# A delta-rule attention with a GELU network behind it: another eviction for one product, other buffers, zero products and a new written order

## The chip, the core and the metric

The kernel runs on one core of a Trainium2 chip. Five engines work side by side and meet through semaphores: TensorE (PE, with its weight loads shown apart as PEld) multiplies from SBUF into PSUM; VectorE (DVE), ScalarE (ACT) and GpSimd (POOL) do elementwise work, the last without PSUM in this kernel; SyncE (SP) issues most DMAs. The metric is the time of one execution on the device in microseconds.

## The reference

For 4 batches and 8 heads, a state of 48 by 48 is carried over 768 steps, and its output goes through two dense layers.

```python
k_n = k / (np.linalg.norm(k, axis=-1, keepdims=True) + 1e-06)
for t in range(S):
    y[:, :, t] = np.einsum('bhd,bhde->bhe', q[:, :, t], state)
    v_old = np.einsum('bhde,bhd->bhe', state, kt)
    state = state + bt * np.einsum('bhd,bhe->bhde', kt, vt - v_old)
...
h = x @ w_in                       # 3072 x 384 by 384 x 2048
g = 0.5 * h * (1.0 + np.tanh(c * (h + 0.044715 * h * h * h)))
return (g @ w_out).astype(np.float32)
```

Inputs and output are float32; the kernel multiplies in bf16 and sums in float32.

## The kernel before

The 768 steps are cut into 12 chunks of 64 steps. A chunk c has two units of work, u = 2c and 2c+1, of 8 head rows each over 128 partitions (two blocks of 64 steps). Within a chunk the recurrence is solved as a triangular system: a 64 by 64 matrix per head is inverted, first in blocks of 8 by substitution, then by doubling. Names are those of the operations in the code; a number behind the point is the unit or the chunk.

- `load` and `norms` (chunk): the DMAs k, q, v; sq (squares of the keys), sum, pow (square root), eps, inv.
- `prep` (unit): kn (keys scaled to tok), qb (queries cast), vb (values cast); knc, qbc, vbc are the same for a whole chunk. T (or Tk, Tq in the first units) transposes them on TensorE and kT (kTk, kTq) copies that out; `turn` does it by a DMA instead. G (GD, GQ) multiplies keys with keys and queries, dn and wq (or wqa and wqb) copy that out.
- `leaf` (chunk): F gathers the blocks of 8, lp scales by beta, x0 starts the inverse, L spreads, six pairs xm and xa on VectorE do the substitution, xb scales.
- `scale` (unit): xe (or xec for two units) spreads the inverses into zt, KZ multiplies the keys with them, kz copies that out, GM multiplies with the keys, lw copies that out under a mask (line 623).
- `invert` (unit): X10 and X11 put lw into the block matrix bd; product A4, eviction rt4 (added to twice the identity, line 704), product B4, evictions bde40 and bde41 (or xi4 and bdc40, bdc41); product A5, the last but one, its eviction rt5 (line 704 too, 128x256), product B5 for the corners, evictions be50 and be51.
- `chain` (chunk): V and K against the state, R copies, U applies the inverse, Un copies, S and Sn make the next state, Q and O the output, On copies, X and xT (or the DMA turnx) transpose it for the dense layers.
- `mlp` (chunk): 16 products `up` (line 824), four `gelu` on ScalarE (line 828), 8 groups `down` (line 835), evictions Z and stores out.

Nothing here is left to a scheduler at run time: `ORDER` is one list, written out, of all operations in order. Each word names an operation, behind the colon the engine (a, d, g, s for ScalarE, VectorE, GpSimd and SyncE; none is TensorE), behind the @ the PSUM bank of eight. `Flow.order` cuts it into one queue for each engine, and every engine works through its queue in that order; `Flow.emit` adds the semaphore waits that the data, the buffers and the banks ask for. A later operation cannot pass an earlier one on its engine, even one that waits. An operation that the list doesn't name is not emitted: several are declared in two ways (`alt`), and the list takes one.

`const` and `preset` write masks, identities, zero pads and templates (two, sel, rows, tri, ladj, bdz); `warm_up` declares 140 zero products named fill, 128x128 by 128x512, which use a tensor wz of zeros and whose result nobody reads; the list names two. Buffers turn over by number: tok, kT and wq have NP = 6 (three chunks), bd 6, lw and zt 4, the raw inputs 3.

## Time and profile before

| what | before |
|---|---|
| median of 3 runs | 254.16 us (254.01 to 254.86) |
| the profiled execution | 256.58 us, span 254.7 us |
| busy: PE, DVE, ACT, POOL | 226.0, 185.8, 157.4, 130.1 us |
| mean granted clock of TensorE | 0.966 |
| matmuls, weight loads | 5500, 5502 |
| instructions of DVE, ACT, POOL | 445, 244, 159 |

The profile is of one execution. A row of groups gives line, engine, operation, written and read tiles, shapes and count, then the busy time and the mean length of one in ns, then how long the engine was idle before them and what ended that. A row of the timeline gives the start, the length, the engine and the count of the instructions merged. A row of waits gives the total, the number and the longest. A row of windows gives the stretch, its length, the busy time and count for PE, PEld, DVE, ACT and POOL, the granted clock of TensorE (1.00 is full), the busy share of the DMA engines and GB/s. The tile `ps` is PSUM, whatever product stands in it. A busy PE is one with a matmul in flight.

### The profile page before, as it was taken

Reading aid. Unit: us, or ns where it says so; the run is one execution under the profiler, and the core shown is the slowest. Engines: PE = TensorE matmul, PEld = TensorE weight load, DVE = VectorE, ACT = ScalarE, POOL = GpSimd, SP = SyncE. Lnnn points to the kernel's source line nnn. Section 1 sums busy time; section 2 is a strip of 40 time slices with the busy share of each in tenths; the row PEclk is TensorE's granted clock in tenths of the full one; section 3 lists DMA queues with packets and bytes.
Section 4 is the critical chain, followed back from the end, with each engine's and each line's share of the span. In section 5 each row is a group of like instructions: output and inputs, shape, how many; then the busy total and the mean of one; then the engine's idle time right before and its main releaser. Section 6 shows DMA issues by size and latency. Waiting matters only on the chain.

```text
span 254.7 us, 12256 instructions
## 1 busy us (share of the span) xinstructions
PE 226.0 (89%) x5500; PEld 178.3 (70%) x5502; DVE 185.8 (73%) x445; ACT 157.4 (62%) x244; POOL 130.1 (51%) x159
## 2 busy tenths in 40 slices
PE   0259558899999998999999899999999999999994
PEld 0148347687877877777778778787786778678672
DVE  6599989955996989898888779898494665755100
ACT  2637747949568888967647577743866534436261
POOL 7647448347563397627358968472535525330000
PEclk9999956689999999999999999999999999999999
DMA  5986995987785679789678517787359320332042
GB/s 103 165 144 118 184 162 95 165 127 117 128 130 105 112 126 124 135 165 147 119 146 167 100 36 131 147 153 130 56 93 167 62 49 4 33 68 64 3 93 62
DMA packets 104532, 28.25 MB, mean 111 GB/s; under 512 B 98592, under 2 KB 103712, under 8 KB 104480
## 3 DMA queue, kind: packets, MB, share of 16 engines
q1 hardware_dynamic: 99200, 23.79, 54.0%
q0 software_dynamic: 2880, 3.15, 7.8%
q8 instruction: 43, 0.70, 1.2%
q10 hardware_dynamic: 2400, 0.54, 1.1%
q14 instruction: 9, 0.07, 0.1%
HBM read 20.64 MB, written 4.72 MB: 100 GB/s over the span
## 4 chain that ended last, share of the span: by engine, by line
PE 73%; DVE 15%; ACT 4%; DMA 2%; ACTq 2%; issue 2%; SPq 1%; POOL 0%
PE ps L835 24%; PE ps L824 22%; PE ps L692 5%; PE ps L620 3%; PE ps L752 3%; PE ps L773 2%; DMA vraw<-in_v_dram 2%; PE ps L697 2%; PE ps L564 2%; DVE lw L623 2%; DVE xl L658 2%; PE ps L633 2%; PE ps L759 2%; DVE ps L655 2%; PE ps L609 1%
## 5 line engine op out<-in xcount | busy, mean ns | idle before, releaser
L824 PE MATMUL ps<-xT,W 128*128 128x256 bf16 x576 | 76.8, 277 | 0.4 <-DVE xl L658 0.4
L835 PE MATMUL ps<-W,gT 128*128 128x384 bf16 x384 | 72.7, 326 | 0.0
L828 ACT ACTIVATE gT<-ps 128x1024 bf16<-128x1024 f32 x48 | 48.4, 1022 | 26.4 <-PE ps L824 25.8
L824 PEld LDWEIGHTS ps<-xT,W 128*128 128x128 bf16 x576 | 52.2, 99 | 9.3 <-DVE xl L658 0.5
L835 PEld LDWEIGHTS ps<-W,gT 128*128 128x128 bf16 x384 | 34.0, 97 | 18.2
L682 POOL TENSOR_SCALAR_AFFINE_SELECT bd<-lw 64x512 bf16<-64x512 bf16 x34 | 22.6, 667 | 37.7 <-DVE lw L623 28.6
L704 DVE TENSOR_TENSOR rl<-ps,two 128x384 bf16<-128x384 f32 (+1 forms) x48 | 22.9, 484 | 9.7 <-PE ps L692 9.5
L623 DVE CAST_PREDICATED lw<-mlw,ps 128x832 bf16<-128x832 uint16 x24 | 24.3, 1018 | 6.8 <-PE ps L620 6.5
L499 POOL TENSOR_TENSOR nrm<-nrm,half 128x16 f32<-128x16 f32 x9 | 26.6, 2956 | 2.8 <-DVE nrm L497 2.7
L343 ACT ACTIVATE bd<-ps 32x256 bf16<-32x256 f32 (+1 forms) x40 | 16.8, 428 | 8.2 <-PE ps L692 4.4
L692 PEld LDWEIGHTS ps<-lw,bd 128*128 128x128 bf16 x384 | 15.5, 98 | 4.2 <-POOL bd L682 1.2
L692 PE MATMUL ps<-lw,bd 128*128 128x32 bf16 (+1 forms) x384 | 17.2, 183 | 1.2 <-POOL bd L682 1.1
L658 DVE TENSOR_TENSOR xl<-ps,xl 128x96 bf16<-128x96 f32 (+4 forms) x72 | 16.0, 228 | 2.0
L655 DVE TENSOR_TENSOR ps<-ps,xl 128x64 f32<-128x64 f32 (+5 forms) x72 | 15.6, 221 | 2.0 <-PE ps L649 0.5
L343 ACT ACTIVATE ob<-ps 128x384 f32<-128x384 f32 x17 | 8.3, 490 | 14.0 <-PE ps L835 14.0
L722 POOL COPY bd<-xi 64x256 f32<-64x256 f32 x20 | 8.0, 401 | 16.4 <-ACT xi L343 8.5
L540 PE MATMUL ps<-ident,tok 128*128 128x128 bf16 x80 | 7.8, 246 | 8.1 <-POOL tok L531 3.8
L531 POOL TENSOR_TENSOR tok<-kraw,nrm 128x384 bf16<-128x384 f32 x9 | 8.5, 945 | 12.7 <-DVE bsb L349 5.6
L349 ACT ACTIVATE kT<-ps 128x512 bf16<-128x512 f32 x18 | 10.4, 596 | 6.4 <-PE ps L609 6.4
L343 ACT ACTIVATE dn<-ps 128x512 bf16<-128x512 f32 x18 | 10.4, 593 | 5.3 <-PE ps L564 5.3
L620 PE MATMUL ps<-kT 48*64 48x56 bf16 (+1 forms) x768 | 11.1, 196 | 2.8 <-ACT kT L349 1.4
L599 POOL TENSOR_TENSOR zt<-xb,blk 128x2048 bf16<-128x2048 bf16 x3 | 10.9, 3642 | 4.1 <-DVE xb L669 3.9
(132 smaller groups left out, 428.3 us busy)
## 6 DMA issues: line engine op xcount, KB each, us to landing
qraw<-in_q_dram SPq DMA_DIRECT2D x48, 96.0 KB, 3.6
vraw<-in_v_dram SPq DMA_DIRECT2D x48, 96.0 KB, 3.5
kraw<-in_k_dram SPq DMA_DIRECT2D x44, 96.0 KB, 3.6
out_dram<-ob SPq DMA_DIRECT2D x22, 192.0 KB, 3.0
W<-in_moe_w_in_dram POOLq DMA_DIRECT2D x2, 768.0 KB, 8.8
W<-in_moe_w_out_dram POOLq DMA_DIRECT2D x2, 768.0 KB, 9.6
kraw<-in_k_dram ACTq DMA_DIRECT2D x7, 48.0 KB, 3.3
out_dram<-ob SPq DMA_DIRECT2D x3, 96.0 KB, 2.2
```

What stands on the lines that cost most here:

```text
L343: return e.activation(out, in_, ACT.Copy) if e is nc.scalar else e.tensor_copy(out, in_)
L499: if e is nc.scalar else e.tensor_tensor(nr[:, 1, hx], nr[:, 0, hx], half[:, hx], ALU.pow), reads=[nrn, "half"] + ["one"] * (c < ROOTS),
L620: ins = e.matmul(P(ps("GM"))[hf(a), o_ + c0:o_ + c1], kT[s][r, y, g, hf(a)], kT[s][r, z, g, C * a + c0:C * a + c1])
L623: A(("dve",), op("lw"), lambda e, P: e.copy_predicated(lw[m][:, :, 0:LW - LB], mlw[:, :, :].rearrange("p w t -> p (w t)")[:, 16:16 + LW - ...
L655: A(("dve",), f"xm{m}.{c}", lambda e, P, m=m, w=w, part=part: e.tensor_tensor(part(P), P(f"L.{c}")[:, off[m]:off[m] + 2 * H * w].rearrange ...
L658: A(("dve",), f"xa{m}.{c}", lambda e, P, m=m, part=part: e.tensor_tensor(xl[y][:, :, m + 1:LB], part(P), xl[y][:, :, m + 1:LB], ALU.add), ...
L682: A(("pool", "dve"), op(f"X1{a}"), lambda e, P, src=lw[m][hf(a), :, LW - C:LW], dst=bd[b_][hf(a), :, hf(a)], a=a: e.affine_select(out=dst, ...
L692: ins = e.matmul(P(name)[:, C * h + c0:C * h + c1], bd[b_][:, h, :], rhs[:, h, :])
L704: A(("dve",), op(f"rt{i}"), lambda e, P, i=i, c0=c0, c1=c1, r_=r_: e.tensor_tensor(r_[:, 0:H, c0:c1], P(ps(f"A{i}")).rearrange("p (h t) -> ...
L824: ins = e.matmul(P(ph)[:, 256 * f:256 * f + 256].rearrange("p (x t) -> p x t", x=2), W1[:, j, 128 * (i + f):128 * (i + f) + 128], x_[:, :, ...
L828: A(("act",), f"gelu{i // 4}.{c}", lambda e, P, i=i, ph=ph: e.activation(g_[:, i:i + 4, :], P(ph).rearrange("p (f t) -> p f t", f=4), ACT. ...
L835: ins = e.matmul(P(po)[:, 0:DM], g_[:, f, 128 * b:128 * b + 128], W2[:, f, :], start=(f == 0), stop=(f == FC - 1))
```

## The change

- Eviction of the last but one product: rt5 no longer adds twice the identity on VectorE. It multiplies by a sign for each partition (`sign`, −1 and 1 in stripes of 32), as an activation with a scale or a tensor_scalar, so it may stand on ScalarE. The new list has 13 of 24 on ScalarE, 11 on VectorE.
- Sums of squares: a second way is declared, sh and si, which halve 48 columns to 24 and 12 on GpSimd, and su, which sums the rest. The new list names `sum` for every chunk, and none of sh, si and su.
- The squares sq themselves: on ScalarE for all 13 in the old list; in the new one 7 on GpSimd, 3 on VectorE, 3 on ScalarE.
- Buffers: tok, kT and wq for 8 units instead of 6; the keys times inverses (kz) go to zT with 5 buffers instead of a third part of kT; the raw betas lie in the output buffers, so the first outputs wait for the transposes of beta; two scratch tensors of a way of `leaf` that no list used are gone.
- Another way for A4 and rt4 (Ai4, rc4), pairs of chunks in `leaf`, and the two beta evictions on either engine are declared; the list names neither Ai4 and rc4 nor pairs.
- 19 zero products instead of 2: one at the very start, the others between unit 4's transposes and the first output product O.0.
- The list is new: order, engines and banks. Among others GpSimd writes rows1 ahead of the first square; bde41 stands on ScalarE 14 times instead of 8, kz 22 instead of 18, xi4 with its two copies is taken for 8 units instead of 12.
- The DMAs of the inputs are the same, with the same shapes; they stand in the list in another order.

Cut to its core; of the list only the stretches that the prediction speaks of:

```diff
--- before.py
+++ after.py
...
-be51.0:d v2.01:s xe.4:d U.0@0 bde41.3:d KZ.4@4 Un.0:a w2.1:g rt4.2:d kz.4:a O.0@6 sum.3:d A5.3@4 On.0:a S.0@2 rt5.3:d GM.4@0 sq.4:a xe.5:d X.0@6
-B4.2@7 lw.4:d Sn.0:a fill85@4 KZ.5@4 xT.0:a sum.4:d X11.4:g bde40.2:a up4.0@2 kz.5:d pow.3:g up0.0@0 bde41.2:a up1.0 X10.4:d tabG:a up2.0 up12.0@6
...
+bdz1:g mmlw:d beta10:a k1.11:s blk1:d pad7:d rowz:d wz:g bdz0:d k0x1.10:a k0x1.01:s tmplz:g fill136@0 tmpl0:g bdz4:d tmpl1:g k0x1.00:a beta01:s one:g
+mln0:g pad4:d pad3:d blk2:g pad1:d k0x1.11:a q0.11:s pad6:d identf:d pad5:g triwq6:d sign0:d low1:d half:d blk3:g tabS:a k1.10:s mmuq:g beta00:a
+muq0:g k1.01:s pad0:g rows1:g k0x0.00:a beta11:s trilw1:a k1.00:s k0x0.10:a k2.10:s sq.0b:g q0.00:s own:g sum.0b:d k2.11:s ident:d betaT0@0 pow.0b:a
...
+fill131@4 mln1:g xa6.0:d fill51@4 xm6.1:d v0.11:s xb.0:d low2:g Tq.3@5 xa6.1:d xe.1:d wqa.1:a betaS2@7 betaC1:a fill44@4 xe.0:d G.4@2 KZ.1@0 kTq.3:d
+wqb.1:g dn.4:a G.5@4 kz.1:a wq.4:d dn.5:a fill132@0 mwp1:g betaC2:d wqa.5:a GM.1@0 xb.1:g fill114@2 lw.1:d v0.00:s wqb.5:g KZ.0@4 F.2@3 kz.0:a Tq.2@2
+tabG:a sign1:d lp.2:d X10.1:d L.2@3 xe.3:d x0.2:d triwq3:a KZ.3@0 ladj4.0:d GM.0@4 xe.2:d kz.3:a fill43@7 fill46@7 xm1.2:d trilw3:a X11.1:g lw.0:d
+KZ.2@0 k5.10:s fill0@7 fill60@7 fill130@7 kz.2:a xa1.2:d kTq.2:a GM.3@4 sign3:d X11.0:g xm2.2:d k3.10:s fill71@7 xa2.2:d betaC3:a fill95@0 xm3.2:d
+lw.3:d ladj5.0:a X10.0:g k4.11:s k4.01:s A4.1@2 xa3.2:d X11.3:g A4.0@4 xm4.2:d k3.01:s fill42@5 rt4.1:d fill109@5 rt4.0:d k3.00:s X10.3:g B4.1@6
+GQ.2@0 xi4.1:a GM.2@4 k4.00:s vb.1:d B4.0@2 ladj5.1:a xa4.2:d lw.2:d bdc41.1:g vb.0:a v1.00:s bde40.0:a bdc40.1:g V.0@6 v2.01:s bde41.0:a wq.2:d
+A4.3@4 X11.2:g A5.1@5 k4.10:s R.0:a A5.0@2 rt5.1:d fill119@0 X10.2:g rt4.3:d v2.11:s rt5.0:a B5.1@5 fill83@6 xm5.2:d B5.0@0 xa5.2:d w2.0:g q4.00:s
+B4.3@1 xm6.2:d be50.0:a A4.2@4 xa6.2:d bde40.3:d be51.0:a be50.1:a be51.1:a rt4.2:d xb.2:g bde41.3:a U.0@6 w2.1:g xe.4:d fill50@4 Un.0:a GQ.3@2 KZ.4@4
+wq.3:d B4.2@1 kz.4:a fill12@0 qb.7:g O.0@6 vbc.1:d GM.4@4 On.0:a lw.4:d sq.3:g X.0@2 S.0@6 xT.0:d A5.3@4 qb.6:g Sn.0:a up4.0@2 xe.5:d up5.0 up6.0
...
+gelu1.2:a up14.2 eps.6:g out00.1:s up15.2 inv.6:d qb.13:d GM.8@2 gelu3.2:a kn.12:g GM.9@0 lw.8:d KZ.10@6 kn.13:g kz.10:a turn.12:s up8.2@4 sq.7:a
+lw.9:d GM.10@6 X10.8:g KZ.11@2 up9.2 kz.11:a up10.2 X11.8:g lw.10:d vb.9:a up11.2 turn.13:s up0.3@2 gelu2.2:a up1.3 sum.7:d GM.11@0 X10.10:g up2.3
...
+Q.11@6 R.11:a up13.10 B5.22@4 be51.23:a up14.10 be50.22:a down10.10@0 be51.22:a U.11@4 down00.10@1 Un.11:d up15.10 down01.10 gelu3.10:a O.11 down02.10
+On.11:a down03.10 X.11@2 Z0.10:d down11.10 xT.11:a down12.10 down13.10 up0.11@2 Z1.10:a up1.11 up4.11@6 out11.10:s up5.11 up2.11 out00.10:s up12.11@0
...
-    NR, NP, NB, NN, NI, NX, NG, NRL = 3, 6, 6, 4, 3, 3, 3, 2
+    NR, NP, NB, NN, NI, NX, NG, NRL, NZ = 3, 8, 6, 4, 3, 3, 3, 2, 5
+    GROUPS = [[0], [1], [2], [3], [4], [5], [6], [7], [8], [9], [10], [11]]
...
-        braw = sb("braw", [32, NC, 2, C], F32)
+        obs = sb("obs", [128, 4, DM], F32)
+        braw = obs[0:32, :, :].rearrange("p n e -> p (n e)").rearrange("p (c y t) -> p c y t", y=2, t=C)
+        ob = [obs[:, 0:2, :], obs[:, 2:4, :]]
...
-        kT = sb("kT", [128, 3, 4, 128], BF16, NP)
+        kT = sb("kT", [128, 2, 4, 128], BF16, NP)
+        zT = sb("zT", [128, 4, 128], BF16, NZ)
...
+            for i_ in range(4):
+                A(("dve",), f"sign{i_}", lambda e, P, i_=i_: e.memset(sign[32 * i_:32 * i_ + 32, :], 1.0 if i_ % 2 else -1.0), writes=[f"sign{i_}"])
...
-                A(("dve",), f"sum.{z}", lambda e, P, sqx=sqx, nr=nr, hx=hx: e.tensor_reduce(nr[:, 0, hx], sqx, AX.X, ALU.add), reads=[sqn], writes=[nrn])
+                A(("dve",), f"sum.{z}", lambda e, P, sqx=sqx, nr=nr, hx=hx: e.tensor_reduce(nr[:, 0, hx], sqx, AX.X, ALU.add), reads=[sqn], writes=[nrn],
+                  alt=(f"sm.{c}", 0) if c else None)
+                if c:
+                    for n_, d_ in (("sh", D // 2), ("si", D // 4)):
+                        A(("pool",), f"{n_}.{z}", lambda e, P, sqx=sqx, d_=d_: e.tensor_tensor(sqx[:, :, 0:d_], sqx[:, :, 0:d_], sqx[:, :, d_:2 * d_], ALU.add),
+                          reads=[sqn], writes=[sqn], alt=(f"sm.{c}", 1))
+                    A(("dve",), f"su.{z}", lambda e, P, sqx=sqx, nr=nr, hx=hx: e.tensor_reduce(nr[:, 0, hx], sqx[:, :, 0:D // 4], AX.X, ALU.add), reads=[sqn], writes=[nrn],
+                      alt=(f"sm.{c}", 1))
...
-            A(EV, op("kz"), lambda e, P: neg(e, kT[s][:, 2, :, :].rearrange("p g (a t) -> p a g t", a=2), P(ps("KZ")).rearrange("p (a r) -> p a r", a=2)[:, :, 0:4 * C].rearrange("p a (g t) -> p a g t", g=4)),
-              frees=[ps("KZ")], writes=[n("kTz")])
+            A(EV, op("kz"), lambda e, P: neg(e, zT[u % NZ][:, :, :].rearrange("p g (a t) -> p a g t", a=2), P(ps("KZ")).rearrange("p (a r) -> p a r", a=2)[:, :, 0:4 * C].rearrange("p a (g t) -> p a g t", g=4)),
+              frees=[ps("KZ")], writes=[f"kTz{u % NZ}"])
...
+                if i == 5:
+                    A(EV, op("rt5"), lambda e, P, r_=r_: scaled(e, r_[:, 0:H, 0:32], P(ps("A5")).rearrange("p (h t) -> p h t", h=H)[:, :, 0:32], sign[:, 0:1]),
+                      reads=[f"sign{i_}" for i_ in range(4)], frees=[ps("A5")], writes=[rn])
+                else:
+                    A(("dve",), op(f"rt{i}"), lambda e, P, i=i, c0=c0, c1=c1, r_=r_: e.tensor_tensor(
                     r_[:, 0:H, c0:c1], P(ps(f"A{i}")).rearrange("p (h t) -> p h t", h=H)[:, :, c0:c1],
-                    two[:, c0:c1].unsqueeze(1).to_broadcast([128, H, c1 - c0]), ALU.add), reads=["two"], frees=[ps(f"A{i}")], writes=[rn])
+                    two[:, c0:c1].unsqueeze(1).to_broadcast([128, H, c1 - c0]), ALU.add), reads=["two"], frees=[ps(f"A{i}")], writes=[rn], alt=(op("a4"), 0) if i == 4 else None)
```

301 lines of the change are left out of this document (151 added, 150 removed).

## The prediction

> **What bounds the kernel now.** I read the page first, its busy shares and its slices.
>
> ```profile
> span 254.7 us, 12256 instructions
> PE 226.0 (89%) x5500; PEld 178.3 (70%) x5502; DVE 185.8 (73%) x445; ACT 157.4 (62%) x244; POOL 130.1 (51%) x159
> PE   0259558899999998999999899999999999999994
> PEclk9999956689999999999999999999999999999999
> ```
>
> A slice is 6.4 us. From the ninth on TensorE is busy throughout; in the first eight, about 51 us, it is not. There are two stages: a head that builds the first chunks and a body in which one matmul follows the other. The view by windows, cut where the clock changes, tells what each is limited by (columns: length, then busy us of PE, PEld, DVE, ACT, POOL, then the granted clock).
>
> ```profile
> 12.70:22.70 10.00, 6.84 (x153) 5.82 (x154) 9.48 (x28) 4.95 (x10) 4.55 (x7) 1.00 0.78 137
> 22.70:32.90 10.20, 5.93 (x186) 4.68 (x184) 9.79 (x35) 7.73 (x16) 5.31 (x10) 1.00 1.00 165
> 32.90:43.10 10.20, 7.63 (x257) 6.88 (x258) 9.14 (x25) 5.40 (x11) 7.29 (x12) 0.50 0.69 117
> 43.10:46.60 3.50, 2.02 (x81) 1.59 (x79) 3.44 (x8) 3.12 (x6) 2.19 (x3) 0.99 0.92 142
> 46.60:49.90 3.30, 2.89 (x105) 2.66 (x103) 3.30 (x5) 3.23 (x6) 0.54 (x1) 0.50 1.22 180
> 49.90:53.40 3.50, 3.50 (x25) 2.48 (x18) 1.65 (x4) 2.27 (x4) 3.07 (x2) 0.50 1.32 204
> 49.90:63.70 13.80, 13.80 (x248) 10.77 (x240) 8.35 (x17) 9.91 (x15) 8.39 (x7) 0.87 0.83 128
> ```
>
> The head is VectorE's: it is busy 35.2 of the 37.2 us from 12.7 to 49.9. The clock of TensorE is whole up to 32.9, halved to 43.1, whole for 3.5 us, and halved again from 46.6 to 53.4. The page has 1.00 from the start, yet in the chain of waits, in order of time,
>
> ```profile
> 9.00 0.56 DVE nrm L497
> ...
> 15.08 0.62 PE ps L540 x4
> ...
> 24.30 0.46 PE ps L540 x8
> ```
>
> four transposes take 0.62 us at 15 and eight take 0.46 at 24, so the 1.00 of the first 20 us is no record of a full clock. It fell at 46.6 after a stretch in which TensorE was busy 2.02 of 3.50 us, and rose at 53.4 after one in which it was busy all the time. In the body VectorE has room: 8.35 of 13.80 us.
>
> Next come the waits of TensorE alone in the body, and its timeline at both ends of the body.
>
> ```profile
> PE ps L620 <- issue: 0.7, 1, 0.7
> PE ps L620 <- DVE lw L623: 0.7, 1, 0.7
> PE ps L824 <- DVE xl L658: 0.4, 1, 0.4
> PE ps L609 <- ACT gT L828: 0.3, 1, 0.3
> PE ps L609 <- POOL zt L602: 0.3, 1, 0.3
> PE ps L795 <- issue: 0.2, 1, 0.2
> ```
>
> ```profile
> 49.94 3.81 PE L824 MATMUL ps<-xT,W 128*128 128x256 bf16 x18
> ...
> 240.91 5.08 PE L824 MATMUL ps<-xT,W 128*128 128x256 bf16 x45
> 245.82 5.36 PE L835 MATMUL ps<-W,gT 128*128 128x384 bf16 x32
> ```
>
> The first product of the dense part (up4.0, line 824) starts at 49.94 and the last matmul ends at 251.2, 201.3 us later, with 2.6 us of waits between. Behind that lie 3.5 us for the last eviction and store. The time is therefore the start of up4.0, plus the matmul work behind it, plus waits, plus 3.5. One more loss is in the first row: 18 products took 3.81 us at half clock, while 45 took 5.08 at the full one, 0.113 each; 18 of these are 2.0 us. So the cold start of the body costs 1.8 us.
>
> This execution took 256.6 us in all, 1.9 more than its span; the median of the runs, 254.16, is 0.5 below the span. I add up in the span and take that 0.5 off at the end.
>
> **The change, part by part.** Matmul work of the body: the new order issues the same products behind up4.0 with A5.3 done ahead of it and KZ.5 behind, and as many changes between 64-row and 128-row products (96 in both by my count of the two lists). The term stays 201.3 − 1.8 = 199.5 us at full clock, the 2.6 us of waits included.
>
> The head. VectorE bounds it, so I count what its queue has ahead of the first product of the dense part.
>
> ```profile
> 13.06 1.96 DVE L531 TENSOR_TENSOR tok<-kraw,nrm 128x384 bf16<-128x384 f32 x1
> ...
> 14.95 0.54 DVE L531 TENSOR_TENSOR tok<-kraw,nrm 128x384 bf16<-128x384 f32 x1
> ```
>
> ```profile
> 12.63 2.05 POOL L382 TENSOR_SCALAR_AFFINE_SELECT rows<-rows 128x1024 bf16<-128x1024 bf16 x1
> ...
> 32.46 1.01 DVE L623 CAST_PREDICATED lw<-mlw,ps 128x832 bf16<-128x832 uint16 x1
> ...
> 34.79 1.02 DVE L623 CAST_PREDICATED lw<-mlw,ps 128x832 bf16<-128x832 uint16 x1 [0.46 <-PE ps L620]
> ```
>
> ```profile
> L495 ACT ACTIVATE sq<-kraw 128x768 f32<-128x768 f32 x11 | 9.2, 838 | 2.0 <-DMA kraw<-in_k_dram 1.9
> L704 DVE TENSOR_TENSOR rl<-ps,two 128x256 bf16<-128x256 f32 x24 | 10.0, 419 | 6.3 <-PE ps L692 6.0
> L349 ACT ACTIVATE kT<-ps 128x512 bf16<-128x512 f32 x18 | 10.4, 596 | 6.4 <-PE ps L609 6.4
> L343 ACT ACTIVATE bd<-ps 32x256 bf16<-32x256 f32 x29 | 10.4, 368 | 3.6 <-PE ps L697 3.1
> L343 DVE CAST bd<-ps 32x256 bf16<-32x256 f32 x19 | 7.7, 409 | 5.5 <-ACT bd L343 3.1 <-PE ps L697 2.1
> L524 POOL TENSOR_TENSOR tok<-kraw,nrm 128x768 bf16<-128x768 f32 x3 | 4.4, 1477 | 6.8 <-PE ps L824 3.9 <-DVE bd L722 2.3 <-DVE nrm L503 0.6
> L602 DVE TENSOR_TENSOR zt<-xb,blk 128x1024 bf16<-128x1024 bf16 x7 | 4.7, 685 | 0.1
> L343 DVE COPY kT<-ps 128x512 bf16<-128x512 bf16 x6 | 2.3, 416 | 0.3 <-PE ps L540 0.2
> L418 DVE TENSOR_SCALAR rl<-tmpl 128x128 bf16<-128x128 bf16 x1 | 0.7, 655 | 0.0
> L343 DVE COPY wq<-tmpl 128x512 bf16<-128x512 bf16 x1 | 0.5, 510 | 0.0
> L343 DVE CAST vb<-vraw 128x384 bf16<-128x384 f32 x2 | 2.2, 1110 | 0.0
> ```
>
> Out of it go the scaling of keys kn.2, to GpSimd (1.96, of which 0.54 is its own time: it ran through the 2.05 us of GpSimd's rows1); three transposed copies, to ScalarE (3 × 0.42); rt5.0, two corner copies and a block copy of unit 3, to ScalarE (0.42 + 2 × 0.41 + 0.75); sum.3, rt5.3 and xe.5, to behind the first product (2.0); a preset of rl (0.90); and constants and zero fills. Together 12.2 us by each one's own length. In come four presets of wq (4 × 0.51), another of rl (0.65), X10.1, casts of v for chunks 0 and 1 (1.11 + 0.64), betaC2, bde40.3, xT.0 from ScalarE, and constants: 11.0 us. The net is 1.2 us less, with rows1 now ahead of the keys, so that kn.2 need not meet it.
>
> Not all of that arrives. The squares of chunk 0 go to GpSimd behind rows1, and I estimate that the first sum starts near 7.9 instead of 9.0; sel then stands ahead of inv.0b, which eats it again. Followed on through VectorE's queue by these lengths, lw.1 comes about 0.6 us earlier than at 32.46 (lw.0 stood at 34.79). But between lw.1 and lw.0 VectorE now has X10.1, xe.3, a preset of rl, xe.2, xm1.2 besides lp.2 and x0.2: 0.4 + 0.69 + 0.65 + 0.69 + 0.3, some 2.7 us more, in place of a zero fill and a wait of together 0.9; xec.1 (1.2) has gone from ahead of lw.1. Unit 0 loses what unit 1 won. Its later steps win a little again: at full clock its products are shorter, but ScalarE gets rt5.0, both corner copies and the block copy of unit 3 ahead of Un.0, 0.40 + 2 × 0.37 + 0.67, where one corner copy (0.37) and one square (0.84) stood. The price of rt5 on ScalarE is not in the trace: between 0.37 (32x256) and 0.60 (128x512), and by the width I take 0.40, about what VectorE takes; 13 of 24 go there, and in the body TensorE's other work hides them, or at worst 0.2 us each where they stand on a path. Bounds for the start of up4.0: 1.2 earlier (the whole net arrives) and 1.0 later (the order around lw.0 stays on the path). I take 0.4 earlier, 49.5, nearer to the middle since both are argued from the same queue.
>
> The 19 zero products. None has a row; a 256-column product takes 0.113 at full clock and 0.21 at half (the two rows above), so one of 512 columns takes 0.22 to 0.45. Seventeen more are 3.7 to 7.6 us of TensorE's time, where TensorE is idle 11.9 of the 37.2 us from 12.7 on. Three stand together while GM.3 waits for lw.0, so they cost nothing there. Six stand directly ahead of A4, B4 and B5 of units 0 and 1; with their cover gone they would cost up to 6 × 0.45 = 2.7. What they can gain is the clock: they add about 0.5 us of work to each stretch of 3.5 us like the one that fell at 46.6. Ends: nothing, and the 1.8 us of the cold body (with the head's part inside the bounds above). I take 1.8.
>
> The Trainium skill, in TensorE: Matmul & The Clock Gate, Part 1, says that the clock halves after at least one idle window of about 3.4 us and is whole again after a busy one. By that rule the clock would not have fallen at 46.6, and the zero products would buy nothing; the rows show it falling there at 2.02 us busy, so the row decides. The stretches of 10.2, 3.5 and 6.8 us are about three, one and two such windows.
>
> Squares of keys. The halving on GpSimd is written, but the order calls sum, not su, in every chunk, so that part does nothing. What does move are ten of thirteen squares, seven to GpSimd and three to VectorE. ScalarE loses 0.84 for each; GpSimd's price lies between that and 1.48 (its product of two inputs, 128x768), and I take 1.48, the row of the same engine. GpSimd is 51% busy, and the square precedes its key scaling by microseconds, so 0 on the path.
>
> Buffers for four chunks, keys times zeros in a tensor of their own, betas and outputs in one buffer: no wait of TensorE in the body names a reuse of these, so 0, and the outputs' new wait is for a transpose of the first 9 us. Loads stand behind fewer reuses on SP's queue, but no wait of TensorE there names a load; 0. The last steps: KZ.10 to GM.10 now has one group of up between (3 × 0.113), against 0.60 for kz.10, and B5.22 to U.11 one of up and one of down (4 × 0.167, from the 32 in 5.36), 1.0, against two corner copies of 0.37 and their handing over. I add 0.3 each, 0.6 in all.
>
> Sum: 49.5 + 199.5 + 0.6 + 3.5 = 253.1 in the span, 1.6 below 254.7. That makes 252.6 against the median of 254.16.
>
> **The rivals.** First, the clock falls in the same way. For it: the zero products make up 0.5 us in 3.5, and TensorE must wait for VectorE all through the head. Also the clock may become whole later than in the 20 to 24 us of before, since the row of products from 19 on is thinner now. Then 1.8 comes back: 254.4, and with the head's gain gone too 254.8. Chance 0.17 for a time within 0.3% (0.76 us, about what this measurement can tell from no change).
>
> Second, and on the other side: GpSimd's squares hold VectorE up. The row of 1.96 us against 0.54 shows a VectorE instruction with two inputs waiting out a GpSimd one. Five squares of 1.48 (sq.3, 6, 9, 10 and 11) stand from up4.0 on, and the new order has VectorE full there: counted by each one's length, 12.7 us lie in the first 12 us behind up4.0, where 8.35 of 13.80 were busy before. If each square costs VectorE 1.4 and VectorE hands on two thirds, 4.7 us come to TensorE: 257.3. It decides from 2.4 us on. Against it: affine selects and casts of GpSimd stood beside VectorE before, and fewer of these are left. Chance 0.25.
>
> The Trainium skill, in SBUF — State Buffer, section SBUF: two separate sides, says that the two engines share a port pair as an exclusive lock, and whoever comes second waits for the whole instruction. The 1.96 us agrees; by that rule this rival is as priced.
>
> Third, the zero products stand in the way and the clock never holds: 1.8 + 2.7 on top, 257.1. Against it: the products behind them wait for VectorE anyway. Chance 0.13.
>
> **How the numbers follow.** The forecast has 0.45. Faster 0.45, same 0.17, slower 0.25 + 0.13 = 0.38. Its own range is 250.9 to 253.4: 0.8 from the head and 0.9 from waits on either side, the upper end where it meets the first rival. For 8 in 10 the range has to take in most of the slower cases: 250.3 to 257.3.
>
> **What would show it.** The granted clock should be whole from about 27 us on to the end, up4.0 should start near 49.5, and 18 products of line 824 there take 2.0 us. TensorE's waits behind it should sum to about 3 us, and VectorE should be busy over 11 of the 12 us behind up4.0. The prediction is wrong if TensorE's waits in the body exceed 5 us, if up4.0 starts after 51, or if the squares on GpSimd come with VectorE instructions of over 1.5 us.

## The result, and the profile after

The changed kernel takes 260.83 us (median of 4 executions, 260.11 to 260.89), the kernel before beside it 254.28. The ratio is 1.0248, with a 95% interval from 1.0222 to 1.0273: slower, and 3.5 us above the upper end of the range. A later set gave 260.37 against 254.40, 1.0248 again.

The head of the page, after:

```profile
span 258.0 us, 12283 instructions
PE 230.4 (89%) x5519; PEld 175.9 (68%) x5519; DVE 187.4 (73%) x447; ACT 167.0 (65%) x266; POOL 120.3 (47%) x142
PE   1287877898999998999999989989999999999994
PEclk9999999999999999999999999999999999999999
```

The clock row is whole, as forecast; the record of the clock begins at 28 us. The view by windows over the stretches that were shown of before (columns: length, busy us and count of PE, PEld, DVE, ACT, POOL, granted clock, DMA share, GB/s):

```profile
32.90:43.10 10.20, 7.66 (x242) 4.94 (x241) 9.86 (x25) 8.44 (x16) 6.35 (x11) 1.00 0.75 139
43.10:46.60 3.50, 2.28 (x83) 1.84 (x82) 2.66 (x8) 2.90 (x8) 3.40 (x5) 1.00 0.90 136
46.60:49.90 3.30, 2.79 (x120) 2.06 (x117) 3.14 (x5) 2.06 (x4) 2.22 (x3) 1.00 1.27 187
49.90:63.70 13.80, 12.88 (x288) 9.98 (x290) 12.01 (x22) 9.11 (x14) 9.48 (x7) 1.00 0.68 114
```

The clock no longer falls at 32.9 or 46.6. Behind 49.9 VectorE is busy 12.01 of 13.80 us, 8.35 before, and TensorE for the first time idles there. The timeline of TensorE at both ends of the body:

```profile
49.51 0.72 PE L856 MATMUL ps<-xT,W 128*128 128x256 bf16 x5
...
249.13 5.36 PE L867 MATMUL ps<-W,gT 128*128 128x384 bf16 x32
```

The dense part starts at 49.51 (before 49.94), where the forecast had it, and the last matmul ends at 254.5 (before 251.2). So the time was lost in the body. In its first 12 us VectorE is busy 10.2, where the forecast wanted over 11. The waits of TensorE there (total, number, longest):

```profile
PE ps L709 <- DVE rl L725: 1.2, 1, 1.2
PE ps L627 <- ACT gT L860: 1.1, 1, 1.1
PE ps L814 <- issue: 0.8, 2, 0.5
PE ps L639 <- issue: 0.5, 2, 0.2
PE ps L709 <- DVE bd L701: 0.4, 1, 0.4
```

With the smaller ones they come to 5.4 us from up4.0 on, against the 2.6 of before.

To see also what hides in stretched products, I gave every product of the body a price, the median time from its start to the next one's by kind (up 0.33, down 0.65, GM 0.27 and so on, 0.09 more where 64-row and 128-row products meet), and took the rest of the time as loss. The prices sum to 193.7 before and 193.9 after. The losses are 6.8 us in the profiled execution of before, 1.7 of them the half clock, and 10.3 after.

### The profile page after: what moved, and what is told of

Same layout as the page of the kernel before. It is cut to its first block, busy times and chain, and to the rows that moved or that the text cites. A ratio compares the mean times of both kernels' runs of the same rounds, so it can differ in the third digit from the quotient of the medians.

```text
span 258.0 us, 12283 instructions
## 1 busy us (share of the span) xinstructions
PE 230.4 (89%) x5519; PEld 175.9 (68%) x5519; DVE 187.4 (73%) x447; ACT 167.0 (65%) x266; POOL 120.3 (47%) x142
## 4 chain that ended last, share of the span: by engine, by line
PE 69%; DVE 17%; POOL 6%; ACT 5%; issue 2%; POOLq 0%
PE ps L867 22%; PE ps L856 19%; PE ps L709 6%; PE ps L639 3%; PE ps L784 3%; DVE lw L642 2%; PE ps L582 2%; PE ps L805 2%; PE ps L714 2%; ACT bd L352 2%; DVE nrm L508 2%; PE ps L655 2%; PE ps L791 2%; DVE zt L620 2%; POOL nrm L517 1%
## 5 line engine op out<-in xcount | busy, mean ns | idle before, releaser
L604 POOL TENSOR_TENSOR wq<-wq,muq 128x512 bf16<-128x512 bf16 x11 | 13.5, 1227 | 9.8 <-ACT wq L352 9.7
L681 DVE TENSOR_TENSOR ps<-ps,xl 128x96 f32<-128x96 f32 (+5 forms) x72 | 15.5, 223 | 2.6 <-PE ps L675 0.9
L358 ACT ACTIVATE zT<-ps 128x512 bf16<-128x512 f32 x22 | 12.6, 594 | 6.9 <-PE ps L627 6.8
L684 DVE TENSOR_TENSOR xl<-ps,xl 128x96 bf16<-128x96 f32 (+5 forms) x72 | 15.6, 225 | 1.6
L725 DVE TENSOR_TENSOR rl<-ps,two 128x384 bf16<-128x384 f32 x24 | 13.0, 552 | 4.6 <-PE ps L709 4.5
L352 ACT ACTIVATE dn<-ps 128x512 bf16<-128x512 f32 x21 | 12.4, 595 | 4.2 <-PE ps L582 3.9
L508 DVE TENSOR_REDUCE nrm<-sq 128x16 f32<-128x768 f32 (+1 forms) x13 | 11.4, 878 | 3.8 <-POOL sq L507 3.8
L352 ACT ACTIVATE obs<-ps 128x384 f32<-128x384 f32 x16 | 7.8, 490 | 9.2 <-PE ps L867 9.1
L352 DVE CAST bd<-ps 32x256 bf16<-32x256 f32 (+1 forms) x25 | 11.8, 475 | 1.5 <-PE ps L709 0.7
L582 PE MATMUL ps<-kT 48*64 48x128 bf16 (+1 forms) x448 | 11.0, 222 | 1.0 <-DVE rl L425 0.5
```

Source lines behind the costliest of these rows:

```text
L352: return e.activation(out, in_, ACT.Copy) if e is nc.scalar else e.tensor_copy(out, in_)
L508: A(("dve",), f"sum.{z}", lambda e, P, sqx=sqx, nr=nr, hx=hx: e.tensor_reduce(nr[:, 0, hx], sqx, AX.X, ALU.add), reads=[sqn], writes=[nrn] ...
L582: ins = e.matmul(o, kT[s][r, y, g, hf(a)], kT[s][r, z, g, hf(a)])
L681: A(("dve",), f"xm{m}{p}.{c}", lambda e, P, m=m, w=w, part=part: e.tensor_tensor(part(P), P(f"L.{c}")[:, off[m]:off[m] + w2 * w].rearrange ...
L684: A(("dve",), f"xa{m}{p}.{c}", lambda e, P, m=m, part=part: e.tensor_tensor(xl_[:, :, m + 1:LB], part(P), xl_[:, :, m + 1:LB], ALU.add), r ...
```

## The experiments

Ratios are to executions of the kernel before on the same chip. Diffs show a few words of the order on each line.

**The clock of the kernel before.** No edit: a second profile.

> The kernel before, unchanged, profiled a second time, to learn whether the clock falls that were counted as 1.8 us to be won belong to its usual executions. Theory A (they were a mark of that one execution, 256.6 us, and the median of 254.2 has none of them): the granted clock stays whole from about 27 us to the end, the 18 products of line 824 at the start of the dense part take 2.0 us instead of 3.81, up4.0 starts near 49, and the span is about 252.3. Rival B (the falls are in every execution, and the 2.4 us between 256.6 and 254.2 lie elsewhere): the clock is at 0.5 again in the stretches from 32.9 to 43.1 and from 46.6 to 53.4, and the 18 products take 3.8 us again. Time in both: 254.2.

254.45 us, ratio 1.0013 (0.9978 to 1.0049). Its profiled execution, at 255.4 us with a clock of 0.966, had both falls again, and up4.0 at 49.8. But these runs list the clock and span of each execution, and they spread: of 23 of the kernel before, five have 0.966 and a span of 253.4 to 254.5, eighteen have 0.971 to 0.980 and a median span of 252.2. A mean of 0.980 over 252 us leaves 10 us at half clock, as long as the first fall alone; 0.966 leaves 17, both in full. One later profile, of the run before_moved below, is such an execution (clock 0.980). Its windows:

```profile
32.90:43.10 10.20, 7.66 (x264) 6.74 (x263) 9.14 (x25) 5.65 (x11) 7.30 (x12) 0.58 0.57 105
...
46.60:49.90 3.30, 2.43 (x106) 1.99 (x107) 3.30 (x5) 3.29 (x5) 0.60 (x1) 1.00 1.23 175
49.90:53.40 3.50, 3.39 (x64) 2.81 (x62) 2.27 (x7) 3.19 (x5) 3.00 (x2) 1.00 1.31 204
```

The first fall lies from 31.3 to 41.5 here, 1.6 us earlier than in the profile of before, and the second, which the forecast wanted to win back, is not there. Both theories were half right: the falls belong to the kernel, but by the mean clocks the second one comes in full only in a fifth of its executions, and both profiles of the kernel before itself were of that fifth.

**The zero products taken out of the changed kernel.**

```diff
 k0x1.01:s tmplz:g
-fill136@0
 tmpl0:g bdz4:d
...
```

Seventeen fills go in this way; fill83 and fill12 stay.

> The changed kernel without 17 of its 19 zero products (two are left, as before). Theory A (the clock of the kernel before did not fall in its usual executions either, so the zero products buy little): within 0.5 us of 260.8, either way. Rival B (they hold the clock up and are worth the 1.8 us that the forecast gave them): 262.6 or more, with the granted clock at 0.5 in a stretch of the head and in the first microseconds of the dense part. Rival C (they stand in the way, 0.22 us each where TensorE has no wait): 258 to 260.

263.75 us, ratio 1.0361 (1.0320 to 1.0402), clock 0.939 to 0.958. Rival B: they hold the clock and are worth 2.9 us, more than the 1.8 of the forecast. The timeline shows it in the start of the dense part:

```profile
53.34 1.44 PE L856 MATMUL ps<-xT,W 128*128 128x256 bf16 x6
```

The windows show it in the clock, which is half from 32.9 to 43.1 as it was before:

```profile
32.90:43.10 10.20, 7.40 (x227) 6.18 (x226) 8.98 (x22) 8.11 (x16) 5.02 (x9) 0.50 0.77 142
```

Without them the new order starts the dense part at 53.34, 3.4 us later than the old one with its own two zero products. Ahead of that start its clock is half for 18.5 us, against 13.6 before, so the 3.4 are the order and the clock together; no run parts the two. The new head needs its zero products, and they hid what the rest of it cost.

**The squares on GpSimd.** The two longest waits have a common neighbour. The timelines of VectorE, GpSimd and TensorE after, around B4.15 and ahead of KZ.19:

```profile
149.67 1.70 DVE L549 TENSOR_TENSOR tok<-kraw,nrm 128x384 bf16<-128x384 f32 x1
151.29 1.64 DVE L620 TENSOR_TENSOR zt<-xb,blk 128x1024 bf16<-128x1024 bf16 x1
...
149.49 1.47 POOL L507 TENSOR_TENSOR sq<-kraw 128x768 f32<-128x768 f32 x1
150.91 1.47 POOL L604 TENSOR_TENSOR wq<-wq,muq 128x512 bf16<-128x512 bf16 x1
...
153.46 0.41 PE L709 MATMUL ps<-rl,bd 128*128 128x64 bf16 x8 [1.19 <-DVE rl L725]
...
170.58 2.40 DVE L617 TENSOR_TENSOR zt<-xb,blk 128x2048 bf16<-128x2048 bf16 x1
...
170.44 1.47 POOL L507 TENSOR_TENSOR sq<-kraw 128x768 f32<-128x768 f32 x1
```

kn.19 takes 1.70 us (0.54 alone) beside sq.10, xe.16 takes 1.64 (0.69 alone) beside the wqb.16 behind it, and xec.9 2.40 (1.2 alone) beside sq.11. rt4.15 and KZ.19 stand behind them. The waits of the page put KZ.19 down to a gelu, which ended at the same moment, 173.14; xec.9 ended at 172.99. The first experiment:

```diff
 A4.15@3 down00.4@7 rt4.15:d
-sq.10:g
 vbc.7:a up15.5 rt4.14:d B4.15@6 turn.19:s gelu3.5:a
+sq.10:a
...
 xa5.9:d On.7:a
+sq.11:a
...
-sq.11:g
 KZ.19@2 gelu1.6:a
```

> The changed kernel with two of its GpSimd squares, sq.10 and sq.11, on ScalarE. In the profile after, kn.19 takes 1.70 us instead of 0.56 and xe.16 1.64 instead of 0.68 beside and behind sq.10, and xec.9 2.41 instead of 1.22 beside sq.11; TensorE stands 1.36 us ahead of B4.15 and 1.13 ahead of KZ.19. Theory A (the squares stretch VectorE's instructions, and VectorE hands it on to TensorE): these two waits go down to 0.3 or less each, xec.9 takes 1.2 again, and the time is 1.5 to 2.5 us less, 258.3 to 259.3. Rival B (the waits are there for another reason, or others come in their place): within 0.5 us of 260.8, with TensorE still standing over 0.8 us at either place or at the next product that needs VectorE.

257.76 us, ratio 1.0127 (1.0079 to 1.0176), 3.1 us below the changed kernel. The losses at the two products fall from 1.36 and 1.13 to 0.16 and nothing, and xec.9 takes its own time again:

```profile
169.49 1.21 DVE L617 TENSOR_TENSOR zt<-xb,blk 128x2048 bf16<-128x2048 bf16 x1
```

Theory A, with more than its 1.5 to 2.5 us. In a later set, with the changed kernel beside it (below), the difference was only 1.5. In the second experiment the squares stay on GpSimd, at other places:

```diff
-rt4.15:d sq.10:g vbc.7:a
+rt4.15:d vbc.7:a
...
-wqb.16:g B4.14@2
+wqb.16:g sq.10:g B4.14@2
...
-pow.10:g v9.00:s
+pow.10:g sq.11:g v9.00:s
...
-up7.6 sq.11:g KZ.19@2
+up7.6 KZ.19@2
```

> The changed kernel with all its squares still on GpSimd, but two of them at other places in GpSimd's queue: sq.10 behind wqb.16 (about 152.4 us, when VectorE reads PSUM: rt4.14, bde40.15), sq.11 behind pow.10 (about 164.4, beside xm1.9 to xa6.9, which read PSUM too). In the profile after, sq.6 ran at 88.52 beside thirteen such small instructions and none of them was stretched. Theory A (only VectorE instructions with both inputs in SBUF, such as kn and xe, are held up by GpSimd's square): xec.9 takes 1.2 us instead of 2.41, the wait of TensorE at KZ.19 goes, that at B4.15 goes below 0.4, and the time is as with the two squares on ScalarE, 257.3 to 258.5. Rival B (a square on GpSimd costs VectorE its 1.2 us wherever it stands): 260 to 261, with rt4, bde40.15 or the xm and xa of chunk 9 stretched by over 0.5 us.

259.70 us, ratio 1.0164 (1.0092 to 1.0236), and neither forecast. xec.9 was free and the wait at KZ.19 gone, but both squares met others of the same sort. Timelines of GpSimd and VectorE:

```profile
150.14 1.78 POOL L507 TENSOR_TENSOR sq<-kraw 128x768 f32<-128x768 f32 x1
164.03 1.46 POOL L507 TENSOR_TENSOR sq<-kraw 128x768 f32<-128x768 f32 x1
...
150.52 1.95 DVE L620 TENSOR_TENSOR zt<-xb,blk 128x1024 bf16<-128x1024 bf16 x1
164.18 1.44 DVE L662 SCALAR_TENSOR_TENSOR xl<-lp,unit 128x112 bf16<-128x112 bf16 x1
165.66 0.27 DVE L681 TENSOR_TENSOR ps<-ps,xl 128x96 f32<-128x96 f32 x1
```

wqb.16 had moved up, and sq.10 with it, to xe.16 (1.95 us), and B4.15 lost 1.29. sq.11 met x0.9, 0.33 us long alone, now 1.44; the chain of xm and xa behind it came as much later, and B4.17 lost 1.12. The instruction after x0.9, which reads PSUM, took its usual 0.27, but it began when the square was over and decides nothing. In the changed kernel itself sq.6 ran from 88.52 to 89.98 beside a row of these, and none was longer than alone:

```profile
88.52 1.47 POOL L507 TENSOR_TENSOR sq<-kraw 128x768 f32<-128x768 f32 x1 [3.48 <-DMA kraw<-in_k_dram]
...
88.68 0.24 DVE L684 TENSOR_TENSOR xl<-ps,xl 128x80 bf16<-128x80 f32 x1
```

So it is not the square alone that costs, but the square, or another product of GpSimd, beside a VectorE instruction with both inputs in SBUF. The Trainium skill, SBUF — State Buffer, section SBUF: two separate sides, names just this pair (two SBUF inputs on VectorE against a GpSimd operation that reads SBUF) and says that the later one waits for all of the earlier. The rows agree: kn, xe, xec and x0 grow by 0.9 to 1.3 us, the instructions with an input in PSUM by nothing.

**The wait for a power.** pow.3 on GpSimd runs from 52.07 to 55.66, VectorE's next instruction is eps.3, and VectorE stands from 54.22 to 55.69; A4.4 and A4.5 then lose 0.31 and 0.61.

```diff
-xT.0:d A5.3@4
+xT.0:d sum.3:d A5.3@4
...
-rt5.3:d KZ.5@6 X11.4:g sum.3:d kz.5:a up0.0@4
+rt5.3:d X11.4:g up0.0@4
...
-up3.0 up7.0
+up3.0 KZ.5@6 kz.5:a up7.0
```

> The changed kernel with sum.3 ahead of xe.5, X10.4 and rt5.3 in VectorE's queue, right behind xT.0 (KZ.5 and kz.5 a few products later to make room). In the profile after, sum.3 starts at 51.05, pow.3 on GpSimd runs from 52.07 to 55.66, and VectorE stands from 54.22 to 55.69 because eps.3 is next in its queue; A4.4 and A4.5 then come 0.31 and 0.61 late. Theory A (VectorE waiting in line for that power is what holds TensorE there): eps.3 waits under 0.4 us, the two losses go below 0.3 together, and the time is 0.6 to 0.9 less, about 260.0. Rival B (VectorE simply has too much to do behind up4.0, so that the work is late whatever its order): A4.4 and A4.5 lose as much as before or the loss moves to U.1, and the time stays within 0.3 of 260.8.

260.85 us, ratio 1.0236 (1.0187 to 1.0284): no gain, though the losses at A4.4 and A4.5 were gone. Another came in their place, in the waits of TensorE:

```profile
PE ps L856 <- DVE rl L355: 1.1, 1, 1.1
```

up0.0 takes over a PSUM bank that rt5.3 frees, and I had put rt5.3 behind the sum. The next two runs combine all that was named so far. Both have the squares on ScalarE and, where not shown, KZ.5 as above.

```diff
-xT.0:d A5.3@4
+xT.0:d X10.4:d sum.3:d A5.3@4
...
-lw.9:d GM.10@6 X10.8:g KZ.11@2 up9.2 kz.11:a
+lw.9:d X10.8:g up9.2 GM.10@6 KZ.11@2 kz.11:a
...
-U.11@4 down00.10@1
+down00.10@1 U.11@4
```

> The changed kernel with the two squares on ScalarE, as in the run before, and three further changes of order: X10.4 and sum.3 ahead of xe.5 in VectorE's queue (so that pow.3 starts some 1.3 us earlier and X10.4 is not late), KZ.5 behind up3.0; GM.10 behind up9.2 and KZ.11 behind GM.10; U.11 behind down00.10. Theory A (the waits seen in the traces add up): from 257.8 the losses of 0.31 + 0.61 at A4.4 and A4.5, of 0.2 to 0.3 at up0.0, of 0.38 at GM.10 and 0.38 at U.11 go, 1.5 to 2.0 us: 255.8 to 256.3. Rival B (what is cleared at one place comes back at the next product that waits for VectorE): 257.3 to 258, with TensorE's losses in the body still at 7.5 us or more above the price of the products. Either way it stays above the 254.1 of the kernel before.

258.14 us, ratio 1.0132 (1.0096 to 1.0167). The losses at GM.10 and U.11 were gone, but rt5.3 was still behind, and up0.0 lost 1.38. The second one mends that and moves wqb.16 away from kn.19:

```diff
-A5.3@4
+A5.3@4 rt5.3:d X10.4:d sum.3:d
...
-sq.9:g v7.00:s
+sq.9:g wqb.16:g v7.00:s
...
-bde40.15:d wqb.16:g B4.14@2
+bde40.15:d B4.14@2
```

> The changed kernel with sq.10 and sq.11 on ScalarE, wqb.16 on GpSimd earlier (behind sq.9, near 140 us, where VectorE reads PSUM or one SBUF tensor), rt5.3, X10.4 and sum.3 in this order ahead of xe.5, KZ.5 behind up3.0, GM.10 behind up9.2 and U.11 behind down00.10. In the two earlier runs that moved sum.3, up0.0 stood 1.2 to 1.4 us for rt5.3, which had been left behind sum.3 and xe.5. Theory A (each wait has the cause that the trace names): up0.0 waits under 0.3, kn.19 takes 0.56 again instead of 1.38, the losses at A4.4, A4.5, GM.10 and U.11 stay away, and the time is 1.4 to 2 us below the run before, which stood 1.3% above the kernel before: 256 to 257, or 0.6 to 0.9% above the kernel before. Rival B (the new order is slow as a whole and the waits only move): 1.2% or more above the kernel before.

259.13 us, ratio 1.0134 (1.0084 to 1.0184). up0.0, GM.10 and U.11 lost nothing now, and kn.19 took 0.56; yet no gain over the squares alone. A4.4 and A4.5 were late again (0.25 and 0.61): pow.3 started 0.8 us earlier, at 51.28, and took 4.13 us, to 55.41. It takes 2.94 before. Beside it stood xe.5 and sq.4, two VectorE instructions with both inputs in SBUF; whether they are the cause I did not try, and pow.5, with 1.05 us of xb.3 and xec.3 beside it, took its usual 2.90.

To have all side by side, the three kernels were run together, without an edit:

> The changed kernel again, beside the next two on the same chip, as their measure: 2.2 to 2.7% above the kernel before.

260.37 us, ratio 1.0248 (1.0223 to 1.0272).

> The changed kernel with sq.10 and sq.11 on ScalarE once more, beside the changed kernel on the same chip. Theory A (the two squares are worth the 3.1 us seen): 1.0 to 1.5% above the kernel before, 2.3 us or more below the changed kernel. Rival B (a part of it was the chip): less than 2 us below the changed kernel.

258.83 us, ratio 1.0181 (1.0151 to 1.0210): the time of rival B, the squares are worth 1.5 us here, against 3.1 before. That the chip made the difference is not shown: both sets of this kernel ran on the chip numbered 1, and their intervals overlap. The squares are worth 1.5 to 3.1 us by these runs.

> The same with wqb.16 earlier and the three waits of the new order taken out (up0.0 and A4.4, GM.10, U.11), on the same chip. Theory A (waits add up, and the chips hid it): 1.5 us or more below sq_act_2. Rival B (what is saved at the waits is lost again where TensorE stands for its instructions, in products whose predecessors now follow faster): within 0.8 us of sq_act_2, with more lost at the boundaries of 256 instructions in its trace.

258.38 us, ratio 1.0157 (1.0132 to 1.0182): 0.45 below, rival B. What it loses now, in the waits of its TensorE:

```profile
PE ps L814 <- issue: 1.3, 2, 1.1
PE ps L639 <- issue: 0.8, 2, 0.4
```

"issue" is a stop with nothing to wait for. That led to the next runs.

**The eviction rt5.** The 13 on ScalarE go back to VectorE, all in this way:

```diff
-rt5.0:a
+rt5.0:d
```

> The changed kernel with all 24 evictions of the last-but-one product (rt5) on VectorE, as before; 13 of them stand on ScalarE in the changed kernel. An rt5 takes 0.47 us on either engine in the profile after, so VectorE gets 6.2 us more and ScalarE as much less. Theory A (the move to ScalarE relieves VectorE where TensorE waits for it): 261.3 to 263. Rival B (it is worth nothing either way, as the forecast had it, since other products cover it): within 0.4 of 260.8. Rival C (on ScalarE it delays the corner copies and gelu): 259 to 260.4.

261.02 us, ratio 1.0213 (1.0136 to 1.0290): rival B, nothing either way that an interval of 2 us to either side can tell.

**Zero products in the kernel before.** If they hold the clock, the old order might gain too.

```diff
+fill11@6 fill12@6 fill13@6 fill14@6 fill15@6
 L.2@3 k3.01:s
...
+fill18@6 fill19@6 fill20@6 fill21@6
 A4.0@1 X11.3:g
...
```

There are 27 of them at eleven places.

> The kernel before with 27 more zero products of 512 columns, placed where TensorE waits in the head (from 25 to 50 us: ahead of Tq.3, T.4, G.5, KZ.1, GM.1, L.2, GM.3, A4.0, U.0, O.0 and KZ.5, one to five each). In the changed kernel 17 of them were worth 2.9 us. Theory A (the clock is kept up, and the head and the first products of the dense part run at the full clock): granted clock 0.99 or more in place of 0.966 to 0.980, up4.0 starts at 49 or earlier, and the time is 0.5 to 2 us less, 252 to 253.6. Rival B (the head waits for VectorE whatever TensorE's clock is): the clock is held but the time stays within 0.4 of 254.1. Rival C (the zero products stand in the way): 254.6 or more.

258.33 us against 254.52, ratio 1.0117 (1.0045 to 1.0188). The clock held but for 3.4 us (0.991 to 0.993), and the kernel got slower, the time of rival C. The dense part starts at 50.9, 1.0 us later than before. The timeline of TensorE has a reason: it stops within A4.1, after two of its eight products, for 2.38 us, with nothing to wait for.

```profile
35.77 0.22 PE L692 MATMUL ps<-lw,bd 128*128 128x48 bf16 x2
38.38 0.31 PE L692 MATMUL ps<-lw,bd 128*128 128x48 bf16 x6 [2.38 <-issue]
```

GM.18 and G.22 stop so for 1.56 and 1.26. What TensorE lacks is its instructions. The DMA part of the page after has them:

```profile
q8 instruction: 43, 0.70, 1.1%
```

43 packets of 16 KB feed 11,120 instructions of TensorE (matmuls, weight loads, 82 for its semaphores), close to 256 for each packet. I counted these instructions ahead of the stops without a cause: in the changed kernel 2240, 4032 and 5568 ahead of three of them; here 960, 8128 and 9409; in all runs with complete records each such stop lies 192 to 195 above a multiple of 256. The next two test whether the count places the stop.

```diff
 xa2.0:d trilw3:g
-fill0@5
 Tq.3@0
...
```

The diff is against the kernel with 27. This one has 19, those ahead of G.5, KZ.1, GM.1, L.2, GM.3 and A4.0.

> The kernel before with 19 more zero products in the head (ahead of G.5, KZ.1, GM.1, L.2, GM.3 and A4.0 only). With 27, the clock was held at 0.991 to 0.993, but TensorE stood still within single products for 2.38 us (in A4.1), 1.56 (GM.18) and 1.26 (G.22) with nothing to wait for in the profile, and the time was 1.2% more. Theory A (these stops come from the fetching of TensorE's instructions, 16 KB or 128 products at a time, and lie where the count of products puts them): with 8 products fewer ahead of the body the stops lie at other products; with no stop over 1 us the time is 252.5 to 254. Rival B (the zero products as such hold TensorE up, by the clock or by their own time): 256 or more again, with the same three products standing.

258.69 us against 255.38, ratio 1.0114 (1.0073 to 1.0155): as slow as with 27, the time of rival B, and over 4 us above that of theory A. The stops at GM.18 and G.22 have moved into groups of down (0.78 and 0.32 us), and a new one of 1.02 us lies in S.8.

```diff
-fill0@5
+fill0@5 fill1@5
 Tq.3@0
...
```

And this has 36, also against the one with 27: one more at each of nine places.

> The kernel before with 36 more zero products in the head, at the same places as the 27 and more of them at each. Theory A (stops by instruction fetch, set by the count of products): the stops over 1 us lie at other products than A4.1, GM.18 and G.22, or are gone, and the time differs from that of 27 zero products by over 1 us in either direction. Rival B (each zero product costs its time): 1 to 2 us above the kernel with 27, 259 to 260, with the same products standing.

260.40 us, ratio 1.0176 (1.0124 to 1.0228), some 1.5 us more than with 27 against the kernel before: by its time rival B, that each zero product costs, is not excluded here, though 8 fewer had saved nothing. The places speak for theory A. The timelines of TensorE, first with 19, then with 36:

```profile
35.73 0.29 PE L692 MATMUL ps<-lw,bd 128*128 128x48 bf16 x5
37.96 0.23 PE L692 MATMUL ps<-lw,bd 128*128 128x48 bf16 x3 [1.94 <-issue]
```

```profile
35.76 0.41 PE L620 MATMUL ps<-kT 48*64 48x56 bf16 x28
38.21 0.25 PE L620 MATMUL ps<-kT 48*64 48x48 bf16 x4 [2.04 <-issue]
```

Ahead of A4.1 stand 15, 18 and 24 zero products. The stop lies after 5 products of A4.1, after 2, and 4 products ahead of it, in GM.3: 3 and 6 products earlier for 3 and 6 more zero products. The stop in GM.18 lies 9 products earlier with 36 than with 27 (after 20 of its products instead of 29), for 9 more zero products. The count of instructions places the stops, as theory A has it; but the first one stayed about 2 us, and no count tried was free of it.

How long it is depends on when the fetch begins. In the kernel with 27 it began at 35.96, 4.1 us behind the first product of the running 256 instructions; the next one, from 39 us on, 1.2 behind. TensorE went on 1.2 us after a fetch was over, at the earliest. The weights W1 flow from 29 to 38 us, so the last run issues their second half later:

```diff
-G.5@6 w1.1:g kTq.2:a
+G.5@6 kTq.2:a
...
-X11.1:g kz.2:a
+X11.1:g w1.1:g kz.2:a
```

> The kernel before with 27 more zero products, as in an earlier run, and with the second half of the weights W1 (768 KB) issued behind X11.1, near 35.7 us, instead of at 29.0. With it at 29.0, TensorE stood 2.38 us in the middle of A4.1, from 36.0 to 38.4; the fetch of its next 16 KB of instructions began only at 35.96, 4.1 us behind the first product of the running 16 KB, while the DMA engines were full; where they were idle (from 39 us on) the next fetch began 1.2 us behind. Theory A (transfers hold the fetch up, and the fetch holds TensorE up): with the weights out of the way the fetch begins before 34.5, TensorE goes through A4.1 with under 0.6 us lost, and the time falls by 0.5 to 2.4 us from that with 27 zero products (which was 1.2% above the kernel before); a stop may come at the next boundary instead, near 42 to 44, where the weights then flow. Rival B (the stop in A4.1 has another cause): it stays at 2 us or more, whenever the weights flow.

266.66 us, ratio 1.0424 (1.0354 to 1.0495), much slower than either theory had it, but on the point in question clear. The fetch began at 33.37, 1.7 us behind, and A4.1 went through in one:

```profile
35.72 0.37 PE L692 MATMUL ps<-lw,bd 128*128 128x48 bf16 x8
```

The stop came at the next boundary, at 43.6, for 1.6 us: there the fetch began 5.4 us behind while the weights flowed. The loss of time is another thing. ScalarE's sq.4 waited 4.28 us for its keys, which now came behind the weights, and xT.0, which the first product of the dense part needs, is queued behind it:

```profile
54.38 0.84 ACT L495 ACTIVATE sq<-kraw 128x768 f32<-128x768 f32 x1 [4.28 <-DMA kraw<-in_k_dram]
```

So no run here took a stop out and got its time back; what the stops cost is read from the traces alone.

**Waits taken out of the kernel before.**

```diff
-GM.9@6 vb.9:a GM.10@2 X10.8:g lw.9:d sq.7:a KZ.11@0 up10.2 v5.10:s up11.2
+GM.9@6 vb.9:a X10.8:g lw.9:d sq.7:a KZ.11@0 up10.2 v5.10:s up11.2 kz.11:a GM.10@2
...
-KZ.20@2 vbc.10:a G.23@4
+vbc.10:a G.23@4 KZ.20@2
...
-GM.20@2 KZ.21@0 lw.20:d U.9@4
+GM.20@2 KZ.21@4 lw.20:d U.9@0
```

> The kernel before with three waits of its body taken out by order alone: GM.10 behind KZ.11, up10.2 and up11.2 (it stood 0.69 us for lw.8), KZ.20 behind G.23 (0.29 for xe.20), and KZ.21 in another PSUM bank, exchanged with that of U.9, Q.9 and G.22 (0.29 for a gelu). Theory A (in the old order, where few products wait for instructions, such waits can be taken out one for one): 0.8 to 1.3 us less, 0.3 to 0.5% below the kernel before, faster than both. Rival B (it comes back at the next wait or instruction fetch): within 0.2%.

253.62 us against 254.40, ratio 0.9981 (0.9955 to 1.0006): 0.8 less by the medians, but the interval still holds no change, so a kernel faster than both is not shown. The three waits are gone from its trace, and the losses in its body are 4.0 us.

The sums over the body, in us (losses above the price of the products, and what of them lies at the boundaries of 256 instructions):

| kernel | up4.0 starts | losses | at boundaries |
|---|---|---|---|
| before, profiled | 49.9 | 6.8 (1.7 half clock) | 2.2 |
| before_moved | 49.6 | 4.0 | 2.1 |
| after, after_again | 49.5, 49.2 | 10.3, 10.6 | 3.1, 2.4 |
| sq_act, sq_act_2 | 49.8, 49.8 | 7.8, 8.2 | 2.7, 2.5 |
| fixed2, fixed2_2 | 49.4, 49.9 | 9.1, 8.6 | 3.9, 4.3 |

## Why the prediction was wrong

The forecast was 252.6; the profiled execution after took 260.1, 0.7 less than the median. Of the 7.5 us between, 4.9 lie in the span (258.0 where the sum had 253.1) and 2.6 in what the sum was set against.

- **The cold start and "I take that 0.5 off at the end".** This step failed. The 1.8 us of the half clock were taken from one profiled execution, and the sum was then set against a median 2.4 below that execution. The median execution has, by its mean clock, at most half of the second fall (0.973 leaves 13.6 us at half clock, 3.4 of them beyond the first fall), and the executions without the full second fall have a span of 252.2 against 254.1, so most of the gain was counted twice. The spread was there to be suspected: one execution at 256.58 beside three at 254.0 to 254.9. The Trainium skill, TensorE: Matmul & The Clock Gate, Part 1, says that the window which judges the clock runs free, so that one kernel meets it at another phase each time; the mean clocks from 0.966 to 0.980 of the kernel before agree, and so does the first fall at 31.3 in one profile and 32.9 in another.
- **"Squares of keys: so 0 on the path."** This step failed, and of the terms of the body it is the largest: 1.36 and 1.13 us in the trace, 1.5 to 3.1 in time. The second rival had the mechanism, and the text's own mark for it, VectorE instructions of over 1.5 us beside a square, came with 1.70, 1.64 and 2.40; but it priced five squares alike. Only two of the five cost TensorE anything, and which two was decided by the VectorE instruction beside them. That xe, xec and kn now stood on VectorE where squares stood on GpSimd could be read from the two orders.
- **The head.** up4.0 was forecast at 49.5 and started at 49.51, for the wrong reasons. The net of VectorE's queue was to win 0.4; without the zero products the new order starts at 53.34. The zero products were sized at 1.8 in the body, with what they do for the head left inside the bounds of up4.0, and measured 2.9 us of time, 3.8 at that start. Two errors of over 3 us cancelled, which was luck. (The third rival's 2.7 takes 0.45 for a 512-column product at half clock; twice the 0.21 beside it is 0.42, so 2.5.)
- **"sum.3, rt5.3 and xe.5, to behind the first product (2.0)."** Counted as a gain of the head. It put pow.3 2.0 us later, and eps.3 at the head of VectorE's queue without its input for 1.5 us: 0.9 us at A4.4 and A4.5 in the trace, though no run got that back in time. What is queued behind eps.3 was not asked.
- **KZ.10 to GM.10 and B5.22 to U.11, 0.3 each.** Right: 0.38 and 0.38.
- **rt5 on ScalarE, 0.** Right as far as the interval tells; it takes 0.47 on ScalarE and 0.48 on VectorE, not 0.40.
- **The matmul work.** Right: 193.7 and 193.9.
- **The clock, whole to the end; TensorE's waits about 3 us.** The first came true; the second was 5.4, over the 5 that the text gave as a mark of being wrong.

Of the losses in the body, 10.3 where about 5.5 were forecast, the two squares are 2.5, the power 0.9, the stops for instructions 0.2 to 1 more than before. The rest are waits of 0.2 to 0.4 at KZ.5, KZ.6, U.3 and U.8, none of which was tried by itself. Why fixed2 gained so little over the squares alone is not settled: its stops at the boundaries grew by 1.2 to 1.8 us, about what was taken out at the waits, but nothing here shows that the one brings the other. With the two squares moved, three of the waits gone and the clock whole, the new order still takes 4 us more than the old one (258.38 against 254.40); the cause of that rest stays open.

## What to carry to other kernels

Before a gain is taken from a profile, see whether the median run has the loss at all: compare the profiled execution's time with the others, and take no gain that the difference already contains. When work is moved to GpSimd, look at what VectorE does at that moment: here it lengthened instructions with both inputs in SBUF by 0.9 to 1.3 us, and those that read PSUM by nothing. And filler products are instructions too: where TensorE runs many short products and weights are flowing, they can bring stops for instruction fetches, as in the kernels with 27 and 36 more here, which got slower though their clock was held.

## What the runs showed of the hardware that I had not expected

TensorE's instructions come in packets of 16 KB, 256 instructions or 128 products with their weight loads, and it can run dry. The next packet's fetch began about 1 to 2.4 us behind a boundary in most places, 2.8 to 5.4 where the weights flowed; it took 0.9 to 1.8 us, and TensorE went on at the earliest 1.2 us later. Added up, an estimate from these rows: 128 products in less than some 3 to 5 us, or 5 to 8 beside the weights, mean a stop, within a product and named "issue" by the profile. In the body this cost about 2 to 5.5 us in the kernels here, and in the head of the kernels with more zero products about 2 more in a single place.
